# One group of value products for blocks with three score visits, in a transformer block with local attention

## The chip, the cores and the metric

The kernel runs on one core of one Trainium2 chip. A core has five engines that run side by side, each through its own list of instructions: TensorE (PE, matmuls), VectorE (DVE), ScalarE (ACT), GpSimd (POOL), and SyncE (SP), which here only issues transfers. They wait for one another through semaphores. The time is the device time of one launch, in microseconds (us); the median of three runs is given. Matmuls write to PSUM, which has eight banks of 2 KB per partition; everything else lives in SBUF.

## What is computed

A pre-normalised attention layer with a memory, and a feed-forward layer behind it, on 2048 rows of 576 numbers (bf16):

```python
h  = x + attention(layernorm(x))
h2 = h + gelu(layernorm(h) @ w1 + b1) @ w2 + b2       # 576 -> 4608 -> 576
```

The attention has 32 heads of 18 numbers. The rows form four segments of 512. In a segment each head does softmax attention with a causal mask inside the segment (`a_dot`), and recalls from a memory of the earlier segments (`a_mem`), which is a running sum over keys and values; the two are mixed by a gate per head, and the memory is updated with the segment's keys and values:

```python
o = g * (phi(q) @ M) / (phi(q) @ z) + (1 - g) * softmax(q @ k.T * scale + mask) @ v
M = M + phi(k).T @ v;  z = z + sum(phi(k))            # phi(t) = t + 1 if t > 0 else exp(t)
```

Then `o @ wo` is added to `x`. `B_x` is not used.

## The kernel before

The rows are worked on in eight chunks `c` of 256, each of two tiles (`qt` or `tl`) of 128; two chunks make a segment. The Python text consists of streams, generators that make operations as their inputs come free: `stream_X` and `stream_P` normalise a tile of x and project it to queries, keys and values; `stream_K` and `stream_M` keep the memory; `stream_A` does attention; `stream_B` projects the attention's result with `wo`, adds x, normalises again; `stream_F1` and `stream_F2` are the two feed-forward matmuls.

The streams only say what the operations are. The order in which each engine runs them is the list `ORDER` at the end, a written-out list of operation numbers; four more tables hold choices that go with it: `PLACE` (which of three PSUM banks a temporary gets), `FLIP` (which operations run on the other one of DVE and ACT), `WHOLE` (see below) and the due times in `LATE`. An engine works strictly through its list; whatever waits holds up all that is behind it on that engine.

Attention goes block by block: a block is a chunk, a tile of queries and half of the heads, `(c, qt, gh)`. A block needs the products of its queries with every tile of keys up to its own in the segment, for four groups of four heads. Sixteen such products of 128 x 128 (four units of four heads) make one score visit: `scores` (L1104, matmuls at L1112) fills the four PSUM banks `st4`, then ACT takes the exponent of all of it into one of three SBUF buffers `pt` (L1129, buffer `v % NT`, `NT` = 3), and POOL sets the part above the diagonal to zero (L1133). Since there is only one `st4`, the next visit has to wait until the exponent has read it. Then `weighted` (L1144, matmuls at L1152) multiplies the exponents by the values and adds into the PSUM bank `ox`; `finish` (L1193) transposes `ox`, takes the reciprocal of the sums (L1197), and writes the attention's result (L1203 in the first segment, L1205 and L1206 later). An exponent cannot be written into a `pt` buffer before the value products that read it are done.

How many visits a block has depends on the place of its queries in the segment: one for `c` even and `qt` = 0, two for `c` even and `qt` = 1, three for `c` odd and `qt` = 0, four for `c` odd and `qt` = 1. There are 80 visits. Value products are made for groups of up to two visits (`PVS` = 2), so a block with three visits has a group of two and a group of one.

Score visits, value products and the last contraction rows of the feed-forward (`tail`, L1385: 64 rows, two at a time) use the array split into parts; all other matmuls use it whole. Two halves of a feed-forward group do their four tails together ahead of the rest of their matmuls (`rest`); for the operations in `WHOLE` the tails are done at full height with the rest (`whole`, through L864 and L865) instead.

In the opening, x tiles are loaded into two buffers `x_p` (L730), DVE takes their statistics (L871, L880) and normalises (L884), and the result is transposed, on PE at first and later by a transposing DMA (L567) into `xT`. While PE has nothing to do at the start it runs warm-up matmuls on a zeroed tile (L1647).

Of the kernel before, what the change touches and what calls it, by code (L numbers as in the profile page):

```python
# [16 lines left out]
def kernel(  # L17
# [88 lines left out]
    ops = []  # L106
# [29 lines left out]
    class Tok(tuple):  # L136
# [22 lines left out]
    }  # L159
    FLIP = {  # L160
# [4 lines left out]
    }  # L165
    WHOLE = {
        2535, 2536, 2537, 2538, 2539, 2541, 2542, 2544, 2548, 2552, 2565, 2569,
# [352 lines left out]
    def op(eng, dur, issue, rd=(), wr=(), slack=0.0, table=None, port=None, mode="full", tag=None):  # L520
# [3 lines left out]
        needs = own_preds(rd, wr)  # L524
        o = Op(eng, dur, issue, preds_of(rd, wr), late[n] if n < len(late) else now + slack, table)
        o.tag = tag, n
        o.toks = [k for k in (*rd, *wr) if isinstance(k, Tok)]
        o.needs, o.keys = needs, (rd, wr)
# [148 lines left out]
    ox = ps.tile([P, 512], F32, name="ox")  # L677
# [466 lines left out]
    def weighted(c, group, opens):  # L1144
# [12 lines left out]
        op("PE", len(group) * 0.22 + 0.015, go, group_keys(c, group), ["ox"], mode="col")  # L1157

    def group_keys(c, group):
        return [k for slot, units in group for k in [("pt", slot, n) for n in range(4)] + value_keys(c, units)]  # L1160
# [46 lines left out]

    def stream_A():
# [12 lines left out]
        group, closed, opens = [], [], True  # L1221

        def values(blk, grp):
            nonlocal opens
            weighted(blk[0], grp, opens)
            opens = blk[3]
# [458 lines left out]
    for p in {h.pair for h in halves.values() if h.pair and h.pair.attached} - kept:  # L1685
        p.parted = True
        o = p.visit
# [26 lines left out]
    for c, jp in sorted(halves):  # L1714
        if jp % 2 == 0 and parted(c, jp // 2):
            rest([halves[c, jp], halves[c, jp + 1]])

    ORDER = [
# [168 lines left out]
```

## Time and profile before

| | us |
|---|---|
| median of 3 runs | 459.54 (459.49 to 460.14) |
| the profiled execution | 459.28 |
| its span in the profile | 457.3 |
| PE busy in the span | 451.2 |
| ACT busy | 328.7 |
| DVE busy | 273.1 |
| POOL busy | 222.8 |

The granted TensorE clock is 1.0 over the whole span. In a row of the order of time the columns are the start, the length, the engine, the line, the operation, what it writes and reads, and how many instructions are merged; in brackets stands how long the engine stood idle before it and who ended that. PE's matmuls overlap: a row's length is that of the matmuls' way through the array, and the pace is read from start to start. In the list of waits the three numbers are the total in us, the number of times, and the longest.

### The profile page before, as it was taken

What the parts mean: (1) busy time and instruction counts of PE and PEld (TensorE: products, weight loads), DVE (VectorE), ACT (ScalarE), POOL (GpSimd) and SP (SyncE); (2) the same over time, 40 slices, a digit from 0 to 9 for tenths busy, and PEclk for the clock granted to TensorE, in tenths of its full rate; (3) what the DMA queues carried; (4) which work ended last, traced back from release to release, by engine and by line L of the source; (5) the groups of instructions that cost most, each with busy time, mean ns of one, the idle gap of its engine ahead of it and who ended that gap; (6) DMA issues with size and microseconds to landing.
All of it is one profiled execution on the core that took longest, in us unless ns stands there. A gap on an engine that the chain in (4) does not pass through costs nothing.

```text
span 457.3 us, 14469 instructions
## 1 busy us (share of the span) xinstructions
PE 451.2 (99%) x6103; PEld 338.7 (74%) x6103; DVE 273.1 (60%) x605; ACT 328.7 (72%) x323; POOL 222.8 (49%) x379
## 2 busy tenths in 40 slices
PE   8989999999999999999999999999999999999997
PEld 6556788676787766777677777777777878888876
DVE  6888898887685688767665686754652212131311
ACT  8878988987688987989689888687745814654300
POOL 5876777577657478775554578654151100000000
PEclk9999999999999999999999999999999999999999
DMA  8699988988386857657777849865547528873012
GB/s 239 158 158 281 248 218 218 240 171 173 122 190 173 220 98 193 158 161 187 147 172 164 211 141 186 212 187 169 178 149 181 159 80 255 193 236 101 27 40 65
DMA packets 112996, 78.39 MB, mean 171 GB/s; under 512 B 47476, under 2 KB 110884, under 8 KB 112932
## 3 DMA queue, kind: packets, MB, share of 16 engines
q1 hardware_dynamic: 112931, 77.48, 67.0%
q8 instruction: 47, 0.77, 0.7%
q14 instruction: 18, 0.14, 0.1%
HBM read 60.09 MB, written 7.08 MB: 147 GB/s over the span
## 4 chain that ended last, share of the span: by engine, by line
PE 94%; DMA 3%; SPq 1%; DVE 1%; issue 0%; ACT 0%; POOL 0%; ACTq 0%
PE bank L1583 23%; PE bank L864 19%; PE bank L1391 17%; PE last L1583 6%; PE st L1112 6%; PE ox L1152 5%; PE bank L865 5%; PE last L1391 4%; PE bank L1385 3%; PE ox L1583 2%; DMA xT<-xn 1%; DMA x_b<-in_A_x_dram 1%; PE bank L1181 1%; PE ox L1391 1%; PE bank L1077 1%; PE bank L1029 1%
## 5 line engine op out<-in xcount | busy, mean ns | idle before, releaser
L1129 ACT ACTIVATE pt<-st 128x2048 bf16<-128x2048 f32 x80 | 150.1, 1877 | 43.2 <-PE st L1112 38.3
L1583 PEld LDWEIGHTS <-hT 128*128 128x128 bf16 x1188 | 111.6, 98 | 27.4 <-issue 0.6
L1583 PE MATMUL bank<-w_sb,hT 128*128 128x288 bf16 (+1 forms) x864 | 121.7, 284 | 0.0
L1133 POOL TENSOR_SCALAR_AFFINE_SELECT pt<-pt 128x512 bf16<-128x512 bf16 x128 | 80.5, 643 | 42.8 <-ACT pt L1129 41.7
L1467 DVE TENSOR_TENSOR hT<-bank,b1T 128x512 bf16<-128x512 f32 x96 | 65.5, 687 | 57.0 <-PE bank L1391 48.9
L1391 PEld LDWEIGHTS <-w1g 128*128 128x128 bf16 x704 | 65.5, 98 | 15.0 <-issue 6.3
L1391 PE MATMUL bank<-xn2T,w1g 128*128 128x256 bf16 x608 | 76.2, 273 | 0.0
L1483 ACT ACTIVATE hT<-hT 128x1536 bf16<-128x1536 bf16 (+4 forms) x25 | 66.3, 2664 | 7.6 <-DVE hT L1467 7.4
L864 PE MATMUL bank<-wqkv,xT 128*128 128x432 bf16 (+2 forms) x256 | 56.0, 341 | 1.5 <-DVE v_aug L998 1.1
L864 PEld LDWEIGHTS <-xT 128*128 128x128 bf16 x392 | 36.0, 98 | 22.5 <-issue 1.6
L1465 ACT ACTIVATE hT<-bank,b1T 128x256 bf16<-128x256 f32 x46 | 19.0, 473 | 23.4 <-PE bank L1391 22.7
L1583 PE MATMUL last<-w_sb,hT 128*128 128x288 bf16 (+1 forms) x252 | 33.6, 277 | 0.0
L1112 PE MATMUL st<-QT,KT 32*128 32x128 bf16 x1280 | 32.2, 217 | 0.3 <-ACT pt L1129 0.3
L1171 POOL TENSOR_TENSOR pq<-ek,pq 128x512 bf16<-128x512 bf16 x24 | 27.8, 1158 | 9.0 <-DVE ek L1169 8.6
L1112 PEld LDWEIGHTS <-KT 32*128 32x128 bf16 x1280 | 18.5, 92 | 15.7 <-issue 12.2
L864 PE MATMUL bank<-xn2T,w1g 128*128 128x256 bf16 (+1 forms) x232 | 29.0, 258 | 0.0
L1196 DVE STREAM_TRANSPOSE ox<-ox 128x512 f32<-128x512 f32 x32 | 23.2, 725 | 7.3 <-PE ox L1152 7.1
L1589 DVE TENSOR_TENSOR ot<-last,hc 128x288 bf16<-128x288 f32 (+1 forms) x7 | 3.1, 437 | 38.2 <-PE last L1583 37.5
L1152 PE MATMUL ox<-pt,v_aug 128*19 128x128 bf16 x1280 | 25.8, 220 | 0.0
L1589 DVE TENSOR_TENSOR ot<-bank,hc 128x288 bf16<-128x288 f32 (+1 forms) x24 | 10.7, 446 | 24.1 <-PE bank L1583 12.2
L1199 POOL TENSOR_TENSOR r<-r,omg 128x16 f32<-128x16 f32 x32 | 7.1, 223 | 34.4 <-DVE r L1197 34.3
L1152 PEld LDWEIGHTS <-v_aug 128*19 128x19 bf16 x1280 | 17.9, 91 | 7.8 <-issue 4.9
(142 smaller groups left out, 697.3 us busy)
## 6 DMA issues: line engine op xcount, KB each, us to landing
w1g<-in_B_w_dram SPq DMA_DIRECT2D x57, 512.0 KB, 4.3
w_sb<-in_B_w_dram SPq DMA_DIRECT2D x6, 864.0 KB, 8.6
wqkv<-in_B_w_dram SPq DMA_DIRECT2D x10, 512.0 KB, 5.1
hd<-h_t SPq DMA_DIRECT2D x16, 288.0 KB, 3.4
hc<-hd SPq DMA_DIRECT2D x32, 144.0 KB, 2.9
w1g<-in_B_w_dram SPq DMA_DIRECT2D x114, 32.0 KB, 3.6
x_b<-in_A_x_dram SPq DMA_DIRECT2D x18, 144.0 KB, 3.2
hT<-in_B_w_dram SPq DMA_DIRECT2D x5, 512.0 KB, 4.5
```

Of the source, the lines that this page charges most:

```text
L864: nc.tensor.matmul(out=out_ap, lhsT=lhsT_of(slice(0, P), k), rhs=rhs_of(slice(0, P), k), start=(k == 0), stop=False)
L865: nc.tensor.matmul(out=out_ap, lhsT=lhsT_of(slice(0, rest), 4), rhs=rhs_of(slice(0, rest), 4), start=False, stop=True)
L1112: nc.tensor.matmul(out=st4[:, i, n * P:(n + 1) * P], lhsT=KTs[(2 * (c - c % 2) + kt) % NK][rows, g, :], rhs=QTs[(2 * c + qt) % NQ][rows, g ...
L1129: op("ACT", 1.88, lambda: nc.scalar.activation(out=pt[:], in_=st4[:], func=ACT.Exp, scale=scale), sk, [("pt", slot, n) for n in range(4)], ...
L1133: op("POOL", 0.65, lambda n=n: nc.gpsimd.affine_select(out=pt[:, :, n * P:(n + 1) * P], in_=pt[:, :, n * P:(n + 1) * P], pattern=[[0, 4], ...
L1152: nc.tensor.matmul(out=ox[32 * i:32 * i + E, (g % 4) * P:(g % 4) * P + P], lhsT=v_augs[(2 * s0 + kt) % NV][:, G * i + g, :], rhs=pts[slot] ...
L1171: op("POOL", 1.16, lambda: nc.gpsimd.tensor_tensor(out=pq[:], in0=e_g, in1=pq[:], op=ALU.add), ["ek"], ["pq"], slack=due("add"))
L1196: op("DVE", 0.73, lambda: nc.vector.transpose(out=ox[:], in_=ox[:]), [], ["ox"], slack=slack)
L1391: nc.tensor.matmul(out=self.acc[:, a, :], lhsT=self.wt[:, k, f:f + P], rhs=xn2T[self.c % 4][:, k, :], start=False, stop=(k == 3), skip_gro ...
L1467: either((0.684, lambda: nc.vector.tensor_tensor(out=dst, in0=acc(), in1=bias, op=ALU.add)), (nj * (0.22 + w * 0.00098), by_act), [b, "b1T ...
L1483: op("ACT", (f1e - f0) * Q * 0.00083 + 0.18, lambda: nc.scalar.activation(out=hT[:, f0:f1e, :], in_=hT[:, f0:f1e, :], func=ACT.Gelu_apprx_ ...
L1583: nc.tensor.matmul(out=bank_of(b)[:, 0:w], lhsT=hT[:, q, tl * P:(tl + 1) * P], rhs=w2_sb[:, q, hs], start=(q == 0), stop=(q == NF - 1))
```

## The change

`weighted` now returns its operation, and `values` in `stream_A` notes the operations of each block in `products`. After the streams have run, each block with `c` odd and `qt` = 0 (three visits) has its two value operations made one: the second one issues the first one's matmuls and then its own, needs what both needed, and whoever needed the first now needs the joint one. The first is left out of `ORDER`. There are eight such blocks. `NT` stays 3, so all three `pt` buffers are read by the joint operation.

With it come a new `ORDER`, with the eight numbers fewer and 28 warm-up matmuls for 30, and new `PLACE`, `FLIP` (81 entries for 74) and `WHOLE` (22 for 12).

```diff
     PLACE = {
-        6: 1, 7: 2, 10: 0, 11: 0, 15: 1, 21: 2, 22: 0, 24: 2, 26: 2, 27: 0, 28: 1, 29: 0, 30: 1, 31: 1, 32: 2, 39: 1,
+        6: 1, 7: 0, 8: 1, 10: 2, 13: 0, 14: 2, 16: 1, 17: 0, 18: 2, 19: 0, 21: 2, 22: 1, 23: 0, 24: 2, 26: 0, 28: 1,
...
     WHOLE = {
-        2535, 2536, 2537, 2538, 2539, 2541, 2542, 2544, 2548, 2552, 2565, 2569,
+        2534, 2535, 2536, 2537, 2538, 2539, 2540, 2541, 2542, 2544, 2548, 2551, 2552, 2553, 2557, 2565, 2567, 2568,
+        2569, 2570, 2571, 2575,
     }
...
-        o.needs, o.keys = needs, (rd, wr)
+        o.needs, o.keys, o.gone = needs, (rd, wr), False
...
-        op("PE", len(group) * 0.22 + 0.015, go, group_keys(c, group), ["ox"], mode="col")
+        return op("PE", len(group) * 0.22 + 0.015, go, group_keys(c, group), ["ox"], mode="col")
...
+    products = {}
+
...
-            weighted(blk[0], grp, opens)
+            products.setdefault(blk[:3], []).append(weighted(blk[0], grp, opens))
...
+    for blk, two in products.items():
+        if len(two) == 2 and blk[0] % 2 == 1 and blk[1] == 0:
+            one, both = two
+            both.issue = lambda first=one.issue, then=both.issue: (first(), then())
+            both.dur += one.dur - 0.015
+            both.needs = [d for d in both.needs if d is not one] + one.needs
+            for o in ops:
+                if one in o.needs:
+                    o.needs = [d for d in o.needs if d is not one] + ([both] if both not in o.needs else [])
+            one.gone = True
+
     ORDER = [
...
```

295 rows, old and new, of tables (FLIP, ORDER, PLACE) are left out of this document.

## The prediction

> **What bounds the kernel.** I read the page first (busy times and the chain that ended last), then the list of TensorE's own waits, then the order of time around the places that the change touches.
>
> ```profile
> span 457.3 us, 14469 instructions
> PE 451.2 (99%) x6103; PEld 338.7 (74%) x6103; DVE 273.1 (60%) x605; ACT 328.7 (72%) x323; POOL 222.8 (49%) x379
> PE 94%; DMA 3%; SPq 1%; DVE 1%; issue 0%; ACT 0%; POOL 0%; ACTq 0%
> ```
> ```profile
> PE st L1647 <- DVE pq L798: 1.3, 1, 1.3
> PE bank L864 <- DVE v_aug L998: 1.1, 2, 0.6
> PE bank L864 <- DMA xT<-xn: 0.4, 1, 0.4
> PE ox L1029 <- DVE qk_pad L995: 0.3, 1, 0.3
> PE st L1112 <- ACT pt L1129: 0.3, 1, 0.3
> ```
>
> TensorE (PE) holds 94% of the chain, and the second list is all the waiting it does: 3.4 us, of which 1.3 is the start. So the time is the sum of PE's own work plus a little over 2 us of waits, and every one of these waits lies in the first 60 us. A change to this kernel can win only PE work or these few waits, and can lose at any place where PE gets a new wait.
>
> PE work has prices that repeat, read as the distance from the start of one row to the start of the next:
>
> ```profile
> 203.29 1.92 PE L1391 MATMUL bank<-xn2T,w1g 128*128 128x256 bf16 x16
> 205.05 0.89 PE L864 MATMUL bank<-wqkv,xT 128*128 128x432 bf16 x4
> ...
> 206.40 0.39 PE L1385 MATMUL bank<-xn2T,w1g 64*128 64x256 bf16 x4
> 206.72 1.92 PE L1391 MATMUL bank<-xn2T,w1g 128*128 128x256 bf16 x16
> 208.48 1.63 PE L1583 MATMUL bank<-w_sb,hT 128*128 128x288 bf16 x12
> 209.95 0.39 PE L1181 MATMUL bank<-pq,MZ_blk 128*128 128x128 bf16 x4
> ...
> 212.82 1.14 PE L1583 MATMUL bank<-w_sb,hT 128*128 128x288 bf16 x8
> 213.89 0.85 PE L1152 MATMUL ox<-pt,v_aug 128*19 128x128 bf16 x48
> 214.67 0.39 PE L1385 MATMUL bank<-xn2T,w1g 64*128 64x256 bf16 x4
> ```
>
> Sixteen matmuls of 256 columns take 1.76, so 0.11 each. Twelve L1583 take 1.47 (0.1225 each), but eight ahead of the value products take 1.07 in place of 0.98: changing the way the array is split costs 0.09. Four half-height tails (L1385, two at a time) take 0.32: two steps of 0.11 and 0.10 for the change back. 48 value products take 0.78. The row 213.89 also shows that a block with three visits is already one stretch of 48 here; going by PE's order that is so in four of the eight such blocks, and the other four have 32 and 16 apart.
>
> **The change, part by part: PE work.** The changed program's PE order can be counted. It has 28 warm-up matmuls in place of 30: the 25 of the first stretch sit 0.21 apart (5.33 up to the next row), so -0.43. It changes the array's split 248 times in place of 264; 16 x 0.093 = -1.5. Only part of that is the merge: four blocks save two changes each, the rest comes from the new order. Ten more pairs of halves (the longer list `WHOLE`) do their four tails at full height: 40 x 0.11 = 4.4 in place of 20 steps of 0.116 = 2.35, so +2.0. The sum is +0.1 us. So the PE work is the same; the planned gain in switches is spent on tails.
>
> The Trainium skill (TensorEngine Tiling (Array Packing), Tiling Modes, Key Properties) states that a change of mode drains TensorE. If each change cost a whole drain (the row's length less its spacing, about 0.16 for L1583), the 16 would be worth 2.6 and the sum below 1.1 lower; the trace shows 0.09.
>
> **The first two three-visit blocks.** Here the merge puts something on PE's path. These are rows of the first such block before, from its third score visit on, and of the tightest pair of visits:
>
> ```profile
> 41.04 0.40 PE L1112 MATMUL st<-QT,KT 32*128 32x128 bf16 x16
> 41.57 1.88 ACT L1129 ACTIVATE pt<-st 128x2048 bf16<-128x2048 f32 x1 [0.21 <-POOL pt L1133]
> 43.13 0.63 PE L1152 MATMUL ox<-pt,v_aug 128*19 128x128 bf16 x32
> 43.52 1.22 POOL L1133 TENSOR_SCALAR_AFFINE_SELECT pt<-pt 128x512 bf16<-128x512 bf16 x2 [0.92 <-ACT pt L1129]
> 43.70 0.40 PE L1112 MATMUL st<-QT,KT 32*128 32x128 bf16 x16
> 44.21 1.88 ACT L1129 ACTIVATE pt<-st 128x2048 bf16<-128x2048 f32 x1 [0.35 <-PE st L1112]
> 44.87 0.40 PE L1152 MATMUL ox<-pt,v_aug 128*19 128x128 bf16 x16
> 45.20 0.90 PE L864 MATMUL bank<-wqkv,xT 128*128 128x432 bf16 x4
> 46.22 0.40 PE L1112 MATMUL st<-QT,KT 32*128 32x128 bf16 x16
> ...
> 54.94 0.40 PE L1112 MATMUL st<-QT,KT 32*128 32x128 bf16 x16
> 55.45 1.88 ACT L1129 ACTIVATE pt<-st 128x2048 bf16<-128x2048 f32 x1
> 57.38 0.41 PE L1112 MATMUL st<-QT,KT 32*128 32x128 bf16 x16 [0.26 <-ACT pt L1129]
> ```
>
> Number the score visits 0 to 79; the block is 6, 7, 8. Visit 8 (41.04) is followed by its exponent (41.57), two masks on POOL (to 44.74) and then its product (44.87): 3.83 from visit to product. Before, the product of 6 and 7 runs at 43.13 without waiting for that, and exponent 9 (44.21), which overwrites the buffer of visit 6, is free to start. After, the one product reads the buffers of 6, 7 and 8, so it waits for the masks of 8, and exponent 9 waits for it. That product is on PE's path, and whatever is behind it in PE's order waits too. In the changed order:
> - visit 8 to product: visit (0.33), three chains of 432 columns (0.92, 0.92, 1.01), visit 9 (0.33): 3.5, against 3.83 needed: wait 0.35.
> - product to visit 10: product (0.78), memory sums (0.31), an output chain (0.61) and transposes (0.54): 2.24. Needed: product 0.85, 0.15 to exponent 9, 1.88, 0.05: 2.9. Wait 0.65. If exponent 9 is not held, this is 0; the buffer list gives no reason for that.
> - visits 7 to 8 and 10 to 11 are 2.25 and 2.23 apart; the last three rows above show that two visits cannot be closer than 2.44 (0.51 to the exponent, 1.88, 0.05). Wait 0.2 and, as a key exponent (L1055, 0.68) stands between exponents 9 and 10 on ACT, 0.25.
> - visits 13 to 14 are 2.10 apart in both programs: the wait at 57.38 stays.
>
> Sum 1.45, bounds 1.0 (the last pair hidden by lags that PE has then) and 1.9. In the second block (9, 10, 11) visit 11 to product is 3.93, just enough; in the six later ones it is 4.5 or more and the product to the next visit leaves room for the exponent. There I price the merge at nothing, covered by this slack; if a block there lost it, it would cost the same 0.65.
>
> **The opening.** The rest of the change is the new order, placements and sides. These rows carry it:
>
> ```profile
> 19.34 0.87 DVE L884 TENSOR_SCALAR xn<-x_p,mv_p,rstd_p 128x576 bf16<-128x576 bf16 x1
> 22.89 0.31 DVE L998 CAST v_aug<-bank 128x144 bf16<-128x144 f32 x1
> 26.85 0.46 DVE L871 BATCH_NORM_STATS2 stats_p<-x_p 128x6 f32<-128x288 bf16 x1 [1.15 <-DMA x_p<-in_A_x_dram]
> 28.06 0.45 DVE L1203 TENSOR_TENSOR o_nat<-ox,r 128x288 bf16<-128x288 f32 x1
> ```
> ```profile
> 21.72 0.42 SPq L730 DMA_DIRECT2D x_p<-in_A_x_dram  x1
> ```
> ```profile
> 28.70 0.41 PE L1152 MATMUL ox<-pt,v_aug 128*19 128x128 bf16 x16
> ...
> 30.58 0.90 PE L864 MATMUL bank<-wqkv,xT 128*128 128x432 bf16 x4 [0.44 <-DMA xT<-xn]
> ...
> 35.94 0.40 PE L1112 MATMUL st<-QT,KT 32*128 32x128 bf16 x16
> ```
> ```profile
> 23.99 6.54 DMA xT<-xn
> ```
> ```profile
> x_b<-in_A_x_dram SPq DMA_DIRECT2D x18, 144.0 KB, 3.2
> ```
>
> Before, visit 6 starts at 35.94, though by the spacings PE had work only up to 33.67: the opening loses 2.27 (the waits of the second list, each with up to 0.17 more that a matmul row's length hides). In the changed order visit 6 would stand at 32.33. What holds it? The third tile's normalisation (L884, 19.34 before, 39th on DVE) becomes the 51st, with 19.5 us of DVE work ahead of it in place of 15.7. DVE hardly idles here, and had done as much at 23.2 (row 22.89), so L884 ends at about 23.6. The next load into the same x_p, at 21.72 before, has to wait for it, and SP stands still behind: 23.6. Behind it in SP's order are the transposing DMA of xT and then two loads. The load takes 3.2 (the median of its size) to 5.1 (21.72 to 26.85): it lands between 26.8 and 28.8, middle 28.0. DVE's L871 waits for it ahead of L1203, as before, so L1203 ends at about 28.9 (28.51 before) and the value product that reuses `ox` starts at 29.1. From there to visit 6 the changed order has 5.7 of PE work (visits 0.33 twice, products 0.33 and 0.56, sixteen L1077 0.60, two 432 chains 0.92, transposes 0.54 and 0.45, an output chain 0.71); xT, issued at 24.1 and 4.5 to 6.5 long, lands just when it is wanted. Visit 6 then comes at 34.85: 1.1 earlier than before, but the opening loses 2.5 against 2.27. Term +0.25; bounds -1.0 (load lands at once) and +1.3 (5.1 and a transposing DMA of 6.5 that starts late).
>
> **Sum.** 0.1 + 1.45 + 0.25 = +1.8. What lies behind the last matmul (2.7 in this execution) is the same in both. The profiled execution took 459.28 with a span of 457.3, the median is 459.54; the difference is put on the median: 461.3.
>
> **Rivals.**
> - Opening and blocks cancel: the load takes 3.2, visit 6 comes at 33.6, the opening loses 1.0 less, the blocks cost 1.2: +0.3, 459.8. For it: 3.2 is the median. Against: before, the same load took 5.1 in this crowd.
> - Faster: PE's order runs through the opening at its own pace, because the loads that stand earlier in SP's order take the queue's crowd away. Place: the value product at 28.70; price -2.1 with visit 6 at 32.5. With the blocks at their lower bound, 0.1 - 2.1 + 1.0 = -1.0: 458.5. It decides only if L1203 ends before 26.8, that is with a DVE that reaches L884 2 us earlier. Against: DVE's work.
> - A later place loses its slack: the new order shifts visits against the long activations (L1483) all along. One or two waits of 0.65 to 1 at such places: +1.5 more, 462.8. Against: before, PE has no such wait after 60 us.
> - The merge does nothing: four blocks are one stretch already. That leaves order effects alone: 0.1 + 0.25 + 0.4 = +0.75, 460.3. Against it the buffers above.
>
> **How the numbers follow.** 0.2% is 0.92 us, about what can be told from no change here: bounds 458.62 and 460.46. Forecast 461.3 (own range 460.6 to 462.1) 0.48; cancelling 0.17; nothing merged 0.10 (half of it slower by the bound, as 460.3 lies near it); later waits 0.12; faster 0.13. Slower: 0.48 + 0.12 = 0.60, and 0.02 of the near one; same 0.17 + 0.08 = 0.25; faster 0.13. The range leaves out the faster case and the end of the later waits: 458.9 to 463.0.
>
> **What would show it.** Right: PE's waits list gains a row for L1152 on POOL's pt or a second and third for L1112 on ACT's pt near 38 to 47 us; visit 6 starts at 34 to 35.5; L871 waits for x_p until about 28; PE stays without waits after 60 us. Wrong: visit 6 before 33; visit 10 less than 2.5 behind the product of 48; or waits over 0.3 after 60 us.

## The result, and the profile after

The kernel after takes 464.25 us (median of four runs, 463.87 to 466.26) against 459.84 beside it: 1.0093 times as long, with a 95% interval of 1.0065 to 1.0121. The profiled execution took 464.02 with a span of 462.3, 5.0 more than the span before. The prediction was 461.3 (458.9 to 463.0): slower as forecast, but by two and a half times as much, and outside the range.

The page after, first its head and the chain that ended last, then the list of TensorE's waits (total, times, longest):

```profile
span 462.3 us, 14468 instructions
PE 452.2 (98%) x6101; PEld 341.2 (74%) x6101; DVE 273.6 (59%) x610; ACT 327.6 (71%) x320; POOL 223.5 (48%) x380
PE 90%; DMA 3%; DVE 2%; SPq 1%; issue 1%; ACT 1%; POOL 0%; ACTq 0%
```
```profile
PE bank L866 <- DVE qk_pad L993: 1.8, 2, 1.3
PE st L1651 <- DVE pq L800: 1.2, 1, 1.2
PE bank L1183 <- DVE hT L1471: 1.2, 1, 1.2
PE bank L909 <- DVE xn L886: 1.0, 1, 1.0
PE bank L866 <- DMA w1g<-in_B_w_dram: 0.8, 1, 0.8
PE bank L866 <- DMA xT<-xn: 0.8, 1, 0.8
PE bank L866 <- DVE QT L1034: 0.3, 1, 0.3
```

PE is still the bound, with nearly the same busy time, but its waits have grown from 3.4 to 7.1. No row for a visit waiting for its exponent is left in the list. What is there are chains that wait for DVE to empty a bank, and for loads. (Lines have moved by two to four: the visit is L1114, its exponent L1131, the mask L1135, the value product L1154.)

PE's busy time by stretch tells where; each row has PE busy, the number of rows, the granted clock, the DMA share and GB/s. Before:

```profile
60.00:200.00 140.00, 140.00 (x2094) 1.00 0.73 175
200.00:240.00 40.00, 40.00 (x608) 1.00 0.72 172
```

After:

```profile
60.00:200.00 140.00, 138.78 (x2078) 1.00 0.71 175
200.00:240.00 40.00, 37.85 (x570) 1.00 0.74 170
```

Before, PE has no gap between 60 and 240. After, 1.22 and 2.15 are missing there.

For all kernels below I add up the same two sums. "Work" is PE's order laid end to end, with each row at the median distance that rows of its kind and of its successor's kind have in the trace before. "Waits" is what the trace has beyond that; single waits over 0.06 are put to their place; the span has another 4.2 ahead of the first matmul and behind the start of the last. In us:

| | work | visits 0 to 5 (to 35) | 35 to 62 | 80 to 90 | 215 to 230 | other places | below 0.06 each | span |
|---|---|---|---|---|---|---|---|---|
| before | 449.30 | 2.42 | 0.33 | 0 | 0 | 0 | 1.00 | 457.3 |
| after | 449.39 | 2.22 | 1.58 | 1.38 | 2.34 | 0.11 | 1.09 | 462.3 |

The 5.0 are +0.1 of work, -0.2 in the opening, +1.25 in the first blocks and +3.8 at places that the prediction left at nothing.

### The profile page after: what moved, and what is told of

Read it like the earlier page. It is cut to its first block, busy times and chain, and to the rows that moved or that the text cites. A ratio compares the mean times of both kernels' runs of the same rounds, so it can differ in the third digit from the quotient of the medians.

```text
span 462.3 us, 14468 instructions
## 1 busy us (share of the span) xinstructions
PE 452.2 (98%) x6101; PEld 341.2 (74%) x6101; DVE 273.6 (59%) x610; ACT 327.6 (71%) x320; POOL 223.5 (48%) x380
## 4 chain that ended last, share of the span: by engine, by line
PE 90%; DMA 3%; DVE 2%; SPq 1%; issue 1%; ACT 1%; POOL 0%; ACTq 0%
PE bank L1587 23%; PE bank L866 21%; PE bank L1395 13%; PE last L1587 6%; PE st L1114 5%; PE bank L867 5%; PE ox L1154 5%; PE last L1395 4%; PE bank L1389 2%; PE ox L1587 2%; DMA xT<-xn 1%; DMA x_b<-in_A_x_dram 1%; PE bank L1183 1%; PE ox L1395 1%; ACT pt L1131 1%
## 5 line engine op out<-in xcount | busy, mean ns | idle before, releaser
L1131 ACT ACTIVATE pt<-st 128x2048 bf16<-128x2048 f32 x80 | 150.1, 1877 | 39.0 <-PE st L1114 28.6
L1587 PE MATMUL bank<-w_sb,hT 128*128 128x288 bf16 (+1 forms) x864 | 123.3, 284 | 0.0
L1135 POOL TENSOR_SCALAR_AFFINE_SELECT pt<-pt 128x512 bf16<-128x512 bf16 x128 | 80.3, 642 | 57.4 <-ACT pt L1131 57.0
L1471 DVE TENSOR_TENSOR hT<-bank,b1T 128x512 bf16<-128x512 f32 x91 | 61.8, 686 | 65.2 <-PE bank L1395 47.8
L1395 PEld LDWEIGHTS <-w1g 128*128 128x128 bf16 x544 | 50.6, 98 | 11.7 <-issue 4.8
L1395 PE MATMUL bank<-xn2T,w1g 128*128 128x256 bf16 x448 | 57.5, 273 | 0.0
L866 PE MATMUL bank<-xn2T,w1g 128*128 128x256 bf16 (+1 forms) x392 | 52.1, 264 | 2.1 <-DVE qk_pad L993 1.3
L866 PEld LDWEIGHTS <-w1g 128*128 128x128 bf16 x400 | 36.5, 98 | 7.9 <-issue 1.5
L1469 ACT ACTIVATE hT<-bank,b1T 128x256 bf16<-128x256 f32 x56 | 23.3, 473 | 17.4 <-PE bank L1395 13.7
L1114 PE MATMUL st<-QT,KT 32*128 32x128 bf16 x1280 | 32.2, 217 | 0.2
L1114 PEld LDWEIGHTS <-KT 32*128 32x128 bf16 x1280 | 18.7, 92 | 17.0 <-issue 13.2
L867 PE MATMUL bank<-xn2T,w1g 128*128 128x256 bf16 (+1 forms) x98 | 25.9, 264 | 0.0
L1154 PE MATMUL ox<-pt,v_aug 128*19 128x128 bf16 x1280 | 25.0, 220 | 0.0
L1208 POOL TENSOR_TENSOR o_nat<-t,t 128x288 bf16<-128x288 f32 x24 | 19.2, 802 | 8.3 <-DVE t L1207 8.3
L1339 POOL TENSOR_TENSOR h_t<-h_t,b_bc 128x576 f32<-128x576 f32 x16 | 20.5, 1281 | 4.7 <-ACT xn L894 2.6
```

The costliest lines, as they stand in the source:

```text
L866: nc.tensor.matmul(out=out_ap, lhsT=lhsT_of(slice(0, P), k), rhs=rhs_of(slice(0, P), k), start=(k == 0), stop=False)
L867: nc.tensor.matmul(out=out_ap, lhsT=lhsT_of(slice(0, rest), 4), rhs=rhs_of(slice(0, rest), 4), start=False, stop=True)
L1114: nc.tensor.matmul(out=st4[:, i, n * P:(n + 1) * P], lhsT=KTs[(2 * (c - c % 2) + kt) % NK][rows, g, :], rhs=QTs[(2 * c + qt) % NQ][rows, g ...
L1131: op("ACT", 1.88, lambda: nc.scalar.activation(out=pt[:], in_=st4[:], func=ACT.Exp, scale=scale), sk, [("pt", slot, n) for n in range(4)], ...
L1135: op("POOL", 0.65, lambda n=n: nc.gpsimd.affine_select(out=pt[:, :, n * P:(n + 1) * P], in_=pt[:, :, n * P:(n + 1) * P], pattern=[[0, 4], ...
L1154: nc.tensor.matmul(out=ox[32 * i:32 * i + E, (g % 4) * P:(g % 4) * P + P], lhsT=v_augs[(2 * s0 + kt) % NV][:, G * i + g, :], rhs=pts[slot] ...
```

## The experiments

Numbers in ORDER are operations in the order in which they are issued. The order that an engine sees follows from it.

### What the merge alone costs

`merge_alone`, on the kernel before (the merge's code stands in the change):

```diff
+    for blk, two in products.items():
...
-        353, 373, 355, 381, 247, 374, 378,
+        353, 373, 355, 247, 374, 378,
...
-        301, 377, 390, 387, 302, 332, 362, 413, 371, 414,
+        301, 377, 390, 302, 332, 362, 413, 387, 371, 414,
...
```

381 is the first product of the first block, 413 the joint one, 387 the exponent of visit 9. The other seven first products go in the same way, and three more exponents move. Only PE's order differs from the kernel before; the other engines run theirs unchanged.

> The kernel before, with the merge as its only edit: in the four blocks where the products of 32 and 16 stood apart, the 32 matmuls move down to stand directly ahead of the 16; the exponents that reuse the first buffer are issued behind them; nothing else moves on any engine. Theory of the prediction (the joint product waits for the last masks, the next exponent waits for the joint product): before, visit 9 would start about 0.56 earlier, its work is done by 44.3, the product of 48 still waits for the masks at 44.74, exponent 9 starts behind it and visit 10 comes 0.65 to 1.15 late; in the second block visit 13 stands directly behind the product and needs exponent 12, which is 1.65 to 2.1 more. With 0.75 saved on eight changes of the split: +2 to +3 us, 461.5 to 462.5, waits of L1114's kind (visit on pt) near 47 and 55. Rival, the merge does nothing but save the changes: -0.7, 458.8, and no new wait.

Measured: 465.71 (465.03 to 467.72), ratio 1.0123 (1.0098 to 1.0149); span 462.9, 5.6 over the kernel before; work 448.88. Its first row of waits, and the three tightest places in time (product, exponent, next visit):

```profile
PE st L1112 <- ACT pt L1129: 5.9, 6, 1.6
```
```profile
54.39 0.85 PE L1152 MATMUL ox<-pt,v_aug 128*19 128x128 bf16 x48
54.90 1.88 ACT L1129 ACTIVATE pt<-st 128x2048 bf16<-128x2048 f32 x1 [2.33 <-PE ox L1152]
...
56.83 0.40 PE L1112 MATMUL st<-QT,KT 32*128 32x128 bf16 x16 [1.59 <-ACT pt L1129]
...
122.68 0.85 PE L1152 MATMUL ox<-pt,v_aug 128*19 128x128 bf16 x48
123.22 1.88 ACT L1129 ACTIVATE pt<-st 128x2048 bf16<-128x2048 f32 x1 [2.88 <-PE ox L1152]
125.14 0.41 PE L1112 MATMUL st<-QT,KT 32*128 32x128 bf16 x16 [1.61 <-ACT pt L1129]
...
298.52 0.85 PE L1152 MATMUL ox<-pt,v_aug 128*19 128x128 bf16 x48
299.03 1.88 ACT L1129 ACTIVATE pt<-st 128x2048 bf16<-128x2048 f32 x1 [1.86 <-PE ox L1152]
300.96 0.41 PE L1112 MATMUL st<-QT,KT 32*128 32x128 bf16 x16 [1.59 <-ACT pt L1129]
```

So the mechanism of the prediction is real and larger than forecast: in the old order the merge costs over 5, and not only in the first two blocks. Where the next visit stands directly behind the joint product, it starts 2.44, 2.46 and 2.44 behind the product's start: 0.51 to the exponent, 1.88, 0.05. These three and the one at 43.93 (0.64) are the four blocks whose products the merge moved together; at 313.40, where no visit of the next block stands ahead of the product, the next one starts 0.78 behind it and waits for nothing. The changes of the split fell from 264 to 260 and work by 0.42, not by eight changes and 0.75. The rival "does nothing" is out. One row answers a smaller point: the exponent starts 0.51 behind the start of a product that lasts 0.85, so it waits for the matmuls that read its buffer and not for all 48.

`merge_spaced` takes `merge_alone` and moves two of these visits behind other work:

```diff
-        881, 866, 870, 900, 847, 882, 1118, 901, 887,
+        881, 866, 870, 847, 882, 1118, 887,
...
-        714, 864, 890, 889, 891,
+        714, 864, 890, 900, 901, 889, 891,
...
```

> The run merge_alone with two score visits moved: those that stood directly behind a joint product, at 125.14 and 300.96 there, each four PE operations (some 2.2 us of chains) later. Theory (a joint product holds the next exponent, and the next visit can start no sooner than 2.44 behind the product's start; 1.66 was lost because only the product's own 0.78 stood between): both waits go down to 0.1 or nothing, 465.71 - 3.2 = 462.5. Rival (the exponents are a chain of their own, the wait only moves on to the next visit): 465 to 465.7, with waits near 127 to 130 and 303 to 306.

Measured: 465.48 (464.5 to 468.13), span 463.1. The two waits of 1.66 to 1.68 became 0.74 at 128.36 and 1.02 at 304.69, at the visits behind. That is between the two expectations: spacing removes some 0.9 and 0.65, and the rest moves on, since the exponents are a chain that was late already. The total hardly fell: 0.82 near 157, most of it for a load of w1g, and 0.28 near 138 came in, which `merge_alone` doesn't have. In the median the two don't differ: ratio 1.012 here, 1.0123 there.

`apart` asks the same of the new order. It takes the merge out of the kernel after:

```diff
-    for blk, two in products.items():
...
-        353, 355, 55, 377, 386, 362, 372, 331,
+        353, 355, 55, 377, 381, 386, 362, 372, 331,
...
-        285, 394, 436, 429, 440, 395, 301, 430,
+        285, 394, 436, 429, 434, 440, 395, 301, 430,
...
```

> The kernel after with the merge undone and its order kept: in each of the eight blocks the first 32 products are issued by themselves ahead of the last visit of the block, the 16 stay where the joint product was. Eight to nine more changes of the split, +0.75. Theory (the new order already leaves the exponent its time behind each joint product, so that in this order the merge costs only the 0.19 at 45.45): 464.25 + 0.55 = 464.8, no other wait changes. Rival (the prediction's 0.35 + 0.65 at the joint product is what the kernel after loses in the first blocks): the waits of the first two blocks shrink by 1.0 and the total falls to 464.0 or less.

Measured: 467.01 (464.73 to 468.36), ratio 1.0139; span of the profile 466.6. The total can't decide here, since this execution lost 1.4 in the opening to a lower granted clock (last section) and 1.92 near 158 to a load. The places can: work rose by 0.85 for eight changes, and the waits of the first blocks stayed, 1.47 in place of 1.58. So in the new order the merge costs next to nothing. The order has put the time in: the joint products of the first two blocks start at 43.01 and 52.18, and the next visits at 45.45 and 55.11, 2.44 and 2.93 later; in the other six blocks it is 3.09 to 6.61.

### What the longer list WHOLE costs

`whole_alone`, on the kernel before:

```diff
-        2535, 2536, 2537, 2538, 2539, 2541, 2542, 2544, 2548, 2552, 2565, 2569,
+        2534, 2535, 2536, 2537, 2538, 2539, 2540, 2541, 2542, 2544, 2548, 2551, 2552, 2553, 2557, 2565, 2567, 2568,
+        2569, 2570, 2571, 2575,
```

> The kernel before, with the longer list WHOLE as its only edit: ten more pairs of halves do their four tails at full height inside their own products, and the ten groups of tails at half height go. Price of the prediction: 40 x 0.11 = 4.4 in place of 20 x 0.116 = 2.35, less the changes of the split that go with the groups where a group stood by itself: +0.2 each, together +1.1 to +2.05, 460.9 to 461.9, spread over the ten places. Rival (the changes saved pay for the tails): 459.8 within 0.3.

Measured: 460.86 against 460.48 beside it, ratio 1.0011 (0.9999 to 1.0022); span 458.4; work 450.23. That is +0.93 of work, 0.093 a pair, with 252 changes of the split in place of 264, and no new wait over 0.16 behind the opening. The prediction's prices give the same: +2.05 for the tails less 12 x 0.093.

### The later places

Rows of the kernel after around 85, SP's first, then DVE and PE; in brackets the idle time ahead of an instruction and what ended it:

```profile
78.24 3.53 SPq L569 DMA_TRANSPOSE xT<-xn  x2
81.83 0.57 SPq L732 DMA_DIRECT2D x_p<-in_A_x_dram  x1
```
```profile
83.10 0.27 PE L867 MATMUL bank<-xn2T,hT 128*128 128x256 bf16 x1
...
84.31 0.29 PE L867 MATMUL bank<-wo_t,xT 128*128 128x288 bf16 x1
...
84.71 0.46 DVE L873 BATCH_NORM_STATS2 stats_p<-x_p 128x6 f32<-128x288 bf16 x1 [1.70 <-DMA x_p<-in_A_x_dram]
...
85.09 0.67 DVE L1471 TENSOR_TENSOR hT<-bank,b1T 128x512 bf16<-128x512 f32 x1
...
85.82 0.38 PE L1183 MATMUL bank<-pq,MZ_blk 128*128 128x128 bf16 x4 [1.22 <-DVE hT L1471]
```

The eviction of 85.09 empties a bank whose chain had ended at 83.37. It stands behind statistics that wait 1.70 for a load, and PE, whose next matmuls need that bank, stands from 84.6 until it is free. The Trainium skill (TensorE: Matmul & The Clock Gate, Architectural detail) says that the queues of ACT and DVE are strictly first in, first out; these rows agree. Before, the load was issued at 76.23, in place of 81.83, and the statistics stood at 90.06, behind the same eviction:

```profile
82.85 0.68 DVE L1467 TENSOR_TENSOR hT<-bank,b1T 128x512 bf16<-128x512 f32 x1
```

`stats_later` (598 is the statistics, 678 the eviction):

```diff
-        323, 677, 554, 598, 649, 633, 678,
+        323, 677, 554, 649, 633, 678,
...
-        653, 631, 654, 670, 644, 663,
+        653, 631, 654, 598, 670, 644, 663,
```

> The kernel after, with one DVE instruction moved: the statistics of x_p that stand at 84.71 (the first half) are issued behind the statistics of h_t (at 86.98) in place of ahead of hT's eviction at 85.09. The load itself stays as late as it is. Theory (a late load held DVE's queue, and with it the eviction that frees a bank for PE): the wait of 1.22 at 85.82 goes, 464.25 - 1.3 = 462.9. Rival (PE is held there by something else, or gets the wait back within the next few us): 464.0 to 464.4, and a wait of over 0.8 on PE between 83 and 95.

Measured: 462.91, ratio 1.0046 (1.0021 to 1.0072); span 459.9. The wait at 85.8 is gone and nothing came in its place between 62 and 219:

```profile
82.90 0.69 DVE L1471 TENSOR_TENSOR hT<-bank,b1T 128x512 bf16<-128x512 f32 x1 [0.40 <-PE bank L867]
...
83.92 0.39 PE L1183 MATMUL bank<-pq,MZ_blk 128*128 128x128 bf16 x4
...
85.23 0.44 DVE L873 BATCH_NORM_STATS2 stats_p<-x_p 128x6 f32<-128x288 bf16 x1
```

The other place of the kernel after, SP, DVE and PE:

```profile
214.83 1.27 SPq L569 DMA_TRANSPOSE KT<-qk_pad  x1
216.19 0.52 SPq L1356 DMA_DIRECT2D w1g<-in_B_w_dram  x1
216.81 0.48 SPq L732 DMA_DIRECT2D x_b<-in_A_x_dram  x1
217.34 1.23 SPq L569 DMA_TRANSPOSE QT<-qk_pad  x1
```
```profile
222.03 0.61 PE L866 MATMUL bank<-xn2T,w1g 128*128 128x256 bf16 x4 [0.78 <-DMA w1g<-in_B_w_dram]
...
223.42 0.61 DVE L993 CAST qk_pad<-bank 128x432 bf16<-128x432 f32 x1 [3.01 <-issue]
...
224.08 0.60 PE L866 MATMUL bank<-xn2T,w1g 128*128 128x256 bf16 x4 [1.33 <-DVE qk_pad L993]
```

The order of time names no releaser for DVE's 3.01. By the buffers it is the transposing DMA of QT, which reads the qk_pad that L993 overwrites and is issued 6.1 ahead of it. The trace bears this out: this DMA lands at 223.34, 6.0 after its issue, and L993 starts 0.08 later; in `stats_later`, `apart` and `after_again` (220.85, 227.48 and 224.38) it also starts 0.08 behind the landing. Before, this DMA was issued 8 us earlier, ahead of the one of KT (223.01 there) and not behind it:

```profile
209.38 1.30 SPq L567 DMA_TRANSPOSE QT<-qk_pad  x1
```

`loads_earlier` (1385 is w1g, 1363 QT, 1502 KT):

```diff
-        1435, 1413, 1398, 1502, 1414, 1399, 1385, 1436, 1400,
+        1435, 1413, 1398, 1385, 1363, 1502, 1414, 1399, 1436, 1400,
...
-        1401, 1651, 2556, 1363, 1439,
+        1401, 1651, 2556, 1439,
```

> The kernel after, with two transfers moved past one on SP: the load of the whole-height part of w1g (216.19) and the transposing DMA of QT (217.34) are issued ahead of the transposing DMA of KT (214.83). Theory (PE's wait of 0.78 at 222.03 is that load landing late; DVE's idle 3.01 before 223.42 is the conversion that may overwrite qk_pad only when the transposing DMA of QT has read it, and PE's 1.33 at 224.08 follows from that): both waits go, 464.25 - 2.1 = 462.1. Rivals: only the first, 463.4; only the second, 462.9; the KT that is now late makes a new wait of a visit, 463.5 or more.

Measured: in the profiled run 462.21 with a span of 460.5; the waits of 215 to 230 fell from 2.34 to 0.28, and DVE's hold to 0.94:

```profile
221.32 0.61 DVE L993 CAST qk_pad<-bank 128x432 bf16<-128x432 f32 x1 [0.94 <-PE st L1114]
```

The median was 464.54 (462.21 to 467.18), ratio 1.011, so the time alone shows nothing: the runs of this kernel differ by more than the 2.1 that the place is worth, and all but the profiled one had a mean clock of 0.996 (last section). The place in the trace decides. The two transfers were not moved one at a time, and the wait for w1g varies by itself: in `stats_later`, where its load stands as late, it was 0.24.

`transfers_only` has these two and the load of x_p (290) earlier on SP, with DVE's order as it was:

```diff
-        573, 551, 628, 597, 604, 581,
+        573, 551, 628, 290, 597, 604, 581,
...
-        618, 586, 619, 290, 592, 621,
+        618, 586, 619, 592, 621,
```

> The kernel after, with three transfers issued earlier on SP and nothing else moved: the two of the run before (part of w1g and the transposing DMA of QT ahead of the transposing DMA of KT, near 215), and the load of x_p of 81.83 ahead of the transposing DMA of xT of 78.24. DVE's order stays, with the statistics of x_p ahead of hT's eviction. Theory (all that PE loses after 60 us comes from transfers that the new order issues late; the place in DVE's queue hurts only while the load is late): no PE wait over 0.3 after 60 us, 464.25 - 3.4 = 460.8. Rival (the place in DVE's queue is what counts, the load lands late wherever it stands, since the queue is crowded): the wait near 85.8 stays at 0.8 or more, 462.

Measured: 462.79, ratio 1.0052 (1.0033 to 1.0071). The wait near 85 fell from 1.38 to 0.31, so it was the lateness and not only the place in DVE's queue; but 0.33 came in next to it, at a chain on the xT whose transposing DMA now stands behind the load. 215 to 230 had 0.50. "No wait over 0.3" was too much: a chain near 154 waited 0.96 for a part of w1g, for which the kernel after has no wait in its profile.

`late_in_before` puts the cause into the kernel before:

```diff
-        289, 572, 551, 290, 573, 590, 628,
+        289, 572, 551, 573, 590, 628,
...
-        592, 619, 460, 586, 593,
+        592, 619, 460, 290, 586, 593,
...
-        323, 649, 570, 678, 624,
+        323, 649, 570, 598, 678, 624,
...
-        664, 694, 642, 598, 658, 683,
+        664, 694, 642, 658, 683,
```

> The kernel before with two instructions moved, so that it has at one place what the kernel after has at 85.82: the load of x_p (76.23) is issued behind the transposing DMA of KT that follows it (78.83 to 81.06), and the statistics that read it stand in DVE's order directly ahead of hT's eviction of 82.85 in place of 90.07. PE's work and order are untouched. Theory (a load that lands after its turn in DVE's order stops the evictions behind it, and PE stops at the next chain that wants the bank): the load lands 4 to 5 behind its issue at about 81.1, DVE stands until 85.5, the eviction ends near 86.1 and the chain of 83.85 into that bank waits: +2 us, 461.5 to 462 on a median of 459.5 to 460.2. Rival (PE has other work or enough banks to go on): +0.3 or less.

Measured: 463.35 (462.75 to 463.71) against 460.44, ratio 1.0066 (1.0048 to 1.0084); the wait is there with the size foretold, 2.01, and work is the same to 0.01:

```profile
80.52 0.53 SPq L730 DMA_DIRECT2D x_p<-in_A_x_dram  x1
...
85.96 0.46 DVE L871 BATCH_NORM_STATS2 stats_p<-x_p 128x6 f32<-128x288 bf16 x1 [1.83 <-DMA x_p<-in_A_x_dram]
86.34 0.67 DVE L1467 TENSOR_TENSOR hT<-bank,b1T 128x512 bf16<-128x512 f32 x1
...
87.06 0.65 PE L864 MATMUL bank<-wo_t,xT 128*128 128x288 bf16 x4 [1.94 <-DVE hT L1467]
```

The rest of its longer time lies in the opening (0.5) and in 0.66 near 61 that no row explains.

### Repairs and repetitions

`repair_all` has everything above and two more moves on DVE:

```diff
-        20, 81, 6, 81, 104, 56, 102, 76, 81, 38, 44,
+        20, 81, 6, 81, 38, 104, 56, 102, 76, 81, 44,
...
-        397, 438, 439, 421, 398, 461, 442, 466, 443, 426, 467,
+        397, 438, 439, 421, 426, 398, 461, 442, 466, 443, 467,
```

> The kernel after with the three transfers issued earlier and, on DVE, three instructions moved out of the way of an eviction: the statistics of x_p near 85 go behind those of h_t, the second normalisation of the opening (7.85) goes ahead of the statistics that wait for x_b (7.47), and the conversion of qk_pad at 55.76 goes ahead of the normalisation that waits for POOL (54.96). Theory (every such wait is a waiting instruction standing ahead of an eviction in an engine's order): -3.5 at the later places, -1.0 at 8.3, -0.6 at 56.4: 459.1, level with the kernel before or a little faster. Rival (the opening is paced by its loads, a wait taken away there comes back at the next load): 460 to 460.7.

Measured: 461.9 (460.14 to 464.44), ratio 1.0023 (1.0007 to 1.0038). In its profile the wait of 1.04 at 8.3 shrank to 0.28, but 0.86 came at the next chain, whose xT DVE copies behind the same statistics that wait for x_b (7.58); the chain starts at 8.49 in place of 8.72. The rival was right about the opening. Two chains waited 1.2 for an xT from its transposing DMA, at 20.6 and 86.7; the second is the price of issuing the load of x_p ahead of it. The longest wait was another: 1.61 near 156, most of it for a load of w1g. This profile is of the 464.44 execution.

`after_again` is the kernel after, unchanged.

> The kernel after, unchanged, on the chip of the runs beside it. Theory: its waits at 85.8, 222 and 224 come again within 0.5, since the order that makes them is fixed; the opening and the waits on w1g's loads (a wait of 0.96 to 1.92 near 154 to 158 stood in three of the last four profiles and not in the first of this kernel) move by up to 2 us with the loads. 464 to 466.

Measured: 467.32 (465.14 to 470.73). The waits at the fixed places came again: 1.87 near 87.5 and 1.49 near 225; the one on w1g near 222 didn't. In the opening it lost 1.5 to a lower granted clock.

`repair_dve` leaves the opening and the load of x_p alone and has the moves of 1385, 1363, 598 and 426, and the output's DMA (970) two loads later:

```diff
-        1008, 1004, 1009, 970, 1011,
+        1008, 1004, 1009, 1011,
...
-        1017, 1033, 1015, 825, 1022,
+        1017, 1033, 1015, 970, 825, 1022,
```

> The kernel after with what has held so far and nothing in the opening: part of w1g and the transposing DMA of QT ahead of the transposing DMA of KT (215); on DVE the statistics of x_p behind those of h_t (85) and the conversion of qk_pad ahead of the normalisation that waits for POOL (55.8); and the output's DMA of 147.96 behind the two w1g loads that follow it. The load of x_p near 82 stays where it is. Theory: -1.35 at 85.8, -2.0 at 222 and 224, -0.6 at 56.4, and up to -1 at 154 where it waits: 460.0 to 460.5. Rival: new waits of over 0.5 elsewhere, 461.5 or more.

Measured: 461.84 (459.6 to 463.61), ratio 1.0027 (1.001 to 1.0045), where the kernel after had 1.0093 and, repeated, 1.016. The profiled execution is the 459.6 one, with a span of 457.9; in it PE's waits are those of the opening, 1.23 in the first blocks and 0.46 at 219.8. What the other eleven lose has no trace.

`repair_tails` takes seven pairs (2537, 2540, 2544, 2552, 2553, 2557, 2567) out of WHOLE again and issues their tails directly ahead of their first product.

> The same as repair_dve, with seven of the 22 pairs taken out of WHOLE: their four tails are done at half height, two at a time, directly ahead of the pair's first product. whole_alone gave 0.093 for a pair the other way round: -0.65 of PE work, 459.4 to 459.9, level with the kernel before. Rival: the change of the split at such a place costs what the tails save, no difference to repair_dve.

Measured: 461.73 (460.54 to 463.36), ratio 1.0028 (1.0013 to 1.0043): no difference. Work fell by 0.31, not 0.65, with twelve more changes for seven groups; the ten groups that `whole_alone` took out had had twelve between them. One wait came back: 1.3 at 221.5, where a group of tails needs the bank that L992 empties, and L992 had stood 1.42.

Two more ask about the clock in the opening. `after_warm` and `repair_warm` are the kernel after and `repair_dve` with ten warm-ups where PE waits at 8.3:

```diff
-        38, 44, 81, 103, 136, 47,
+        38, 44, 81, 103, 81, 81, 81, 81, 81, 81, 81, 81, 81, 81, 136, 47,
```

> The kernel after with ten more warm-up matmuls (L1651), directly ahead of the transposes of the second tile that stand at 8.32 to 8.60. At 0.11 each they lie in the wait that PE has there. Theory (the wait near 8.5 is long enough that the granted clock falls to 0.5 for some 3 us, which the repetition of the kernel after showed from 8.6 to 12.0 and which costs 1.4 to 1.6): the clock stays at 0.999 or more in every run and the time goes to 463.9 to 464.5. Rival (the clock falls for another reason, or the repetition was slow through its loads alone): mean clocks of 0.996 and less in half the runs, 465 or more.

> The run repair_dve with the same ten warm-up matmuls. Three of its twelve runs had a mean clock of 0.996 and lay 1.5 to 2 above the others. Theory: no run below 0.999, median 461.0 to 461.6, what is left over the kernel before (460.4 beside it) is the variation of the loads. Rival: 461.8 as without them.

Measured: 466.51 (463.15 to 467.62), ratio 1.0137, and 461.82 (459.95 to 463.64), ratio 1.0029. Two of four runs of the first still had a mean clock of 0.996, and one of twelve of the second. So ten warm-ups there don't keep the clock up for sure, and the repairs don't gain by them. The profile of `repair_warm` has a new wait of 1.31 at 236.3, where a chain needs a bank that DVE empties at L1593.

None of the versions beats the kernel before. Those with the later places repaired come within 0.3% of it.

## Why the prediction was wrong

By its own steps, after against before:

| step | forecast | measured |
|---|---|---|
| PE work | +0.1 | +0.09 |
| opening | +0.25, visit 6 at 34.85, L871 released near 28 | -0.2, visit 6 at 34.50, the same statistics at 27.75 |
| first two blocks | +1.45 | +1.25 |
| six later blocks | 0 | 0 |
| PE without waits after 60 us | 0 | +3.8 |

The step that failed is the last one, "PE stays without waits after 60 us". It was argued from the merge alone (do the later joint products have slack?), and that half is right in the new order. The other half of the change, the new order of SP's and DVE's queues, was costed in the opening only. Behind 60 us I counted PE's instructions and never walked the transfers. The rival "a later place loses its slack" had the sign, but priced one or two waits at 0.65 to 1, from long activations. It was three waits of 0.85 to 1.49: a load that PE itself waited for (0.85, which the repetition didn't have), and two kinds of held queue, a DVE instruction that waits for a late load ahead of an eviction (`stats_later`, `late_in_before`), and a conversion that waits for a late transposing DMA to have read its buffer (`loads_earlier`). That the trace before shows no wait there was used as evidence against; but it shows the old order's slack, which was what the change altered: the statistics of x_p stood at 90.06, 7 us behind the same eviction, and now stand ahead of it.

The blocks came out near the forecast by luck. Three of the four waits in the sum were mis-sized: of their 1.45 only 0.38 came, and waits that were not in the sum made up for the rest. Rows of the first block after:

```profile
41.97 1.23 POOL L1135 TENSOR_SCALAR_AFFINE_SELECT pt<-pt 128x512 bf16<-128x512 bf16 x2 [0.49 <-ACT pt L1131]
42.68 0.40 PE L1114 MATMUL st<-QT,KT 32*128 32x128 bf16 x16
43.01 0.85 PE L1154 MATMUL ox<-pt,v_aug 128*19 128x128 bf16 x48
43.52 1.88 ACT L1131 ACTIVATE pt<-st 128x2048 bf16<-128x2048 f32 x1 [0.40 <-PE ox L1154]
...
45.45 0.41 PE L1114 MATMUL st<-QT,KT 32*128 32x128 bf16 x16
```

- "Visit 8 to product: wait 0.35" is not there. The masks end at 43.20 by the profile, and the product starts at 43.01: only its last 16 matmuls read the buffer of visit 8, and they come 0.56 later. The whole group does not wait for the last buffer.
- "Product to visit 10: needed 2.9, wait 0.65" is 2.44 and 0.19. I let the exponent wait for the end of the group and 0.15; it waits for the first buffer's matmuls and starts at 0.51.
- "Visits 7 to 8: 0.2" is 0.19. Visits 10 to 11 have no wait of their own, since PE lost 0.32 at 46.11 for a bank between them.
- Not in the sum at all: that 0.32, 0.20 at 48.86, and 0.68 at 56.41, where the conversion that frees a bank stood on DVE behind a normalisation that waited for POOL. With the two moved past each other (`repair_dve`) the 0.68 is gone and 0.33 came in behind it.

The opening came out near by luck too. The forecast had PE stand at the value product until 29.1, since the late load of x_p would hold L1203 (now L1205). DVE's side came as forecast (the statistics at 27.75, L1205 done at 28.57), but the product started at 28.72 without a wait, 0.27 behind the last matmul of the chain ahead of it, as at 25.20. PE had lost its time earlier: 1.04 at 8.32, where the normalisation of the second tile (7.85 on DVE) stands behind statistics that wait for x_b (7.47), and 0.93 at 20.36 for an xT. Before, the transposes of both tiles ran from 6.59 on without a wait. So the first held queue of the new order was in the opening already.

Three smaller readings were wrong. The two warm-ups that were left out stood in the second stretch, 0.11 apart (four from 7.29 on before, the fourth at 7.62), not 0.21, and after, PE waits directly behind that stretch: the -0.43 was no gain. The merge saves four changes of the split (`merge_alone`), not eight. And half of the chance of "nothing merged" was to count as slower, but 0.02 of its 0.10 was.

In the old order the same merge costs 5.6 (`merge_alone`); in the new one, nothing that `apart` could give back. So the new order does cover the merge: it spends its freedom on putting 2.4 us or more between a joint product and the next visit. And it loses 3.7 at 85, 222 and 224.

Open is how large the loss is in a typical run. The profiled executions of the result and of the repetition account for 5.0 and 6.1, of which 1.5 in the latter is the clock. Runs up to 470.7 have no trace. Two things vary from execution to execution and were in no term of the prediction. The mean clock was 0.996 or less in 16 of the 49 executions of the new order with its opening (`after`, `after_again`, `stats_later`, `loads_earlier`, `transfers_only`, `apart`, `repair_dve`, `repair_tails`) and in 4 of 71 of the kernel before; where a trace has it, it costs 1.4 to 1.5. All four runs of `after_again` were among them, and one of the four of the result. And the wait for w1g near 154 to 158 was 0 in the result, 0.10 in the repetition, 0.96 in `transfers_only`, 1.61 in `repair_all` and 1.92 in `apart`.

## What to carry to other kernels

When a change comes with a new order, walk every queue that it reorders to its end, the DMA queue and the evicting engine first: for each instruction that waits for a transfer, see when that transfer is now issued and which eviction stands behind it. A lack of waits in the old trace says nothing about the slack of a new order. And a group of matmuls over several buffers holds each buffer only until its own matmuls have read it, so where the first buffer stands in the group decides how long the next producer waits.

## What the runs showed of the hardware

The granted clock fell to half in the opening of some executions. In the repeated kernel after, PE's stretches (busy, rows, granted clock, DMA share, GB/s) and the rows ahead of them were:

```profile
6.00:8.00 2.00, 0.71 (x8) 1.00 1.00 319
8.00:10.00 2.00, 1.50 (x8) 0.65 0.81 203
10.00:12.00 2.00, 2.00 (x7) 0.50 1.01 294
12.00:14.00 2.00, 2.00 (x15) 1.00 0.65 201
```
```profile
8.50 0.67 PE L909 MATMUL bank<-ident,xn 128*128 128x128 bf16 x5 [1.45 <-DVE xn L886]
8.97 1.65 PE L866 MATMUL bank<-wqkv,xT 128*128 128x432 bf16 x4
```

Four matmuls of 432 columns took 1.65 there and 0.90 at full clock. The stretch of half clock lasts from about 8.6 to 12.0; one such stretch makes the mean clock over the span 0.996. The Trainium skill (TensorE: Matmul & The Clock Gate, What's actually happening) gives a free-running window of about 3.4 us and the low clock after an idle window; the length agrees, but PE was not idle for a window here: it waited 0.34 and 1.45 and worked in between. The wait alone doesn't decide it either: in `loads_earlier` PE waited 1.53 at the same place and kept the full clock, in `apart` it waited 1.55 and lost it.
